# Where the first MLP's activation lives and which engine makes its low half, in tiles 3 to 5

## The chip, the cores and the metric

One core of a Trainium2 chip. The metric is the device time of one execution in microseconds (us), the median of several runs.

## What is computed

An attention layer (4 batches, 8 heads, 576 positions, head size 64, causal, with a bias from a running sum) gives 2304 rows of 512 numbers. Two MLPs follow. What matters here is the first:

```python
h = x @ w_in                                          # 512 -> 2048
g = np.maximum(h, 0.0) + np.log1p(np.exp(-np.abs(h)))
return (g @ w_out).astype(np.float32)                 # 2048 -> 512
```

The second MLP has the same shape, with a rational function of h in place of g.

## The kernel before

Every product is made to fp32 accuracy from three matmuls of rounded operands. An operand is split into a high half (a rounded copy) and a low half (the rest), and the products high-high, high-low and low-high are summed. So each activation needs both halves before the second product of the MLP can start.

The 2304 rows of the first MLP are cut into six tiles (`T1`, line 17): T = 0 and 1 have 256 rows, T = 2 to 5 have 448. The hidden dimension has 16 blocks `ff` of 128. A unit is one block of one tile. For the first MLP (`ph == 0`) a unit passes through these steps:

- `stage_a_` (L650 to L665): 12 matmuls (L662, L663, L664) write h, 128 x 448, into one bank of PSUM. `hsel` (L669) names the ring the bank comes from. There are eight banks: four `acc`, two `h`, two `at` (L92).
- `stage1_` (L743 on): ScalarE takes |h|, its exponential and its logarithm into the SBUF tile `e` (L749 to L751, two buffers). VectorE adds max(h, 0) and writes the sum over `e` (L752). With this instruction the bank of h is free.
- `stage3_` (L783): ScalarE rounds `e` into `gh` (L788), and GpSimd subtracts: `gl` = `e` - `gh` (L789). Both have three buffers.
- `stage_b` (L684): three units later, 12 matmuls (L698, L699, L700) multiply `gh` and `gl` with the second weight and add into the four `acc` banks. In the tile T = 5 two of the four are taken from `at` (`open_acc`, L675).

Beside this run two other streams. Attention is one list of steps (`s1`, `s2`, `t1`, `t2`, `pv`), of which `gap` (L900) emits a share with each unit; the last of it belongs to the units of T = 3. It takes its banks from `at`. In a step VectorE reduces the scores and adds the mask (L300, L306, L309), ScalarE exponentiates (L313), VectorE makes the reciprocal of the sum (L314, L315), GpSimd multiplies with it (L316, tiles `PA` and `P`), TensorE transposes (L377, L388, L393), and ScalarE and VectorE split the result into halves (L363, L364). L283 and L284 make low halves of q and k; in the last segment of attention L284 is put on GpSimd. In T = 4 and 5 the weights of the second MLP are converted (`conv2_a`, `conv2_b`), one per unit in T = 4: a DMA brings 64-bit numbers (`raw`), GpSimd scales them (L532), VectorE puts the bits together in `tc` (L533, L534, L535), ScalarE rounds them (L539), GpSimd subtracts (L540). `raw` and `tc` have two buffers each. `split_x_` (L632) makes the halves of a tile's input, `xs`.

Each engine works through its own instructions in a fixed order. That order comes from a list scheduler, which goes by program order and by the priorities set with `ahead` and `early` (`PRIO`, `P_ST1`, `P_ST3` and others, L45 to L52). The units of the first MLP that the change touches are these:

```python
units += [(ph, T, ff) for ph in range(2) for T in range(2 - 2 * ph, 6) for ff in range(NF)]
```

Of the kernel before, what the change touches and what calls it, by code (L numbers as in the profile page):

```python
# [12 lines left out]
ALU = mybir.AluOpType  # L13
# [16 lines left out]
H_ONLY = 5  # L30
# [25 lines left out]
def moe_chain_kernel(ctx, tc, qk0, qk, vv, s0, s, w1, w2, ab, out):  # L56
    nc = tc.nc
# [31 lines left out]
    def tmp_tile(tag, bufs, shape=(128, TMAX), dt=F32):  # L89
        return sb.tile(list(shape), dt, tag=tag, bufs=bufs, name=tag)  # L90
# [10 lines left out]
    def early(by_region):  # L101
        return ahead(by_region[region[0]])

    def f(ap):
        return ap.bitcast(F32)
# [544 lines left out]
    def stage_a_(u):  # L650
        ph, T, ff = u
        bk = bank(hsel(ph, T, ff))
        n = TILES[ph][T][1]
        h = bk[:, 0:n]
        if ph == 0:
            wh, wl = w1_t[ff][:, 0:512], li_t.pop((T, ff, 0))
        else:
            wh, wl = w2_t[ff, 0]
        for k in range(KD):
            xh, xl = xs_t[ph, T, k]  # L660
            cs = slice(k * 128, (k + 1) * 128)
            nc.tensor.matmul(h, wh[:, cs], xh, start=(k == 0), stop=False)  # L662
            nc.tensor.matmul(h, wh[:, cs], xl, start=False, stop=False)  # L663
            nc.tensor.matmul(h, wl[:, cs], xh, start=False, stop=(k == KD - 1))  # L664
        h_t[u] = h  # L665
# [1 line left out]
    hcnt = [0]  # L667

    def hsel(ph, T, ff):  # L669
        if ph == 0 or (T == 0 and ff < H_ONLY):  # L670
            return "h"
        hcnt[0] += 1
        return ("h", "at")[hcnt[0] % 2]
# [62 lines left out]

    e_t = {}

    def stage1(u):
        with early(P_ST1):  # L740
            stage1_(u)

    def stage1_(u):  # L743
        ph, T, ff = u
        h = h_t[u]
        n = TILES[ph][T][1]
        if ph == 0:
            e = tmp_tile("e", 2)[:, 0:n]
            nc.scalar.activation(e, h, AF.Abs)  # L749
            nc.scalar.activation(e, e, AF.Exp, scale=-1.0)  # L750
            nc.scalar.activation(e, e, AF.Ln, bias=1.0)  # L751
            nc.vector.scalar_tensor_tensor(e, h, 0.0, e, op0=ALU.max, op1=ALU.add)  # L752
            e_t[u] = e
        else:
            a = tmp_tile("e", 2)[:, 0:n]
            t = tmp_tile("PA", 3, (128, n))
            w = tmp_tile(*(("P4", 1), ("tc", 2), ("tmp", 1), ("tc", 2))[(T * NF + ff) % 4], (128, n))
            nc.scalar.activation(a, h, AF.Abs)
            nc.scalar.activation(w, a, AF.Identity, scale=babs[:, 1:2], bias=babs[:, 0:1])  # L759
            nc.scalar.activation(t, h, AF.Identity, scale=nega[:, 3:4], bias=nega[:, 2:3])  # L760
            nc.gpsimd.tensor_tensor(w, w, a, op=ALU.mult)  # L761
            nc.vector.tensor_tensor(t, t, h, op=ALU.mult)
            nc.vector.scalar_tensor_tensor(t, t, nega[:, 1:2], h, op0=ALU.add, op1=ALU.mult)
            e_t[u] = (a, t, w)
# [14 lines left out]
    def stage3(u):  # L779
        with early(P_ST3):  # L780
            stage3_(u)

    def stage3_(u):  # L783
        g = e_t.pop(u)
        n = TILES[u[0]][u[1]][1]
        gh = tmp_tile("gh", 3, dt=F32R)[:, 0:n]
        gl = tmp_tile("gl", 3, dt=F32R)[:, 0:n]
        nc.scalar.activation(gh, g, AF.Copy)  # L788
        nc.gpsimd.tensor_tensor(gl, g, f(gh), op=ALU.subtract)  # L789
        g_t[u] = (gh, gl)  # L790


    if True:
# [129 lines left out]
        for i in range(NU + LAGS[1]):  # L923
            at_bank[0] = second_bank if i < 8 + LAGS[0] else at_only
            u = units[i] if i < NU else None
            region[0] = 0 if i < 32 else 1 if i < 96 else 2
            if u is not None:
                ph, T, ff = u
                if ph == 0 and T == 0:
                    conv1_to(c1_pos[ff, 0] + 1)  # L930
                stage_a(u)
                gap(i, 0)
                stage1(u)
                with ahead(C2_OFF):
                    while c2_open:
                        conv2_b()
                if ph == 0 and T == 0:
                    e = HF - 1 if ff < HF else NF - 1
                    conv1_to(c1_pos[min(ff + 2, e), 0] + 1)
                    if ff >= e + 1 - HF:  # L940
                        conv1_to(c1_pos[ff, 1] + 1)
                    if ff == e:
                        conv1_to(c1_pos[e, 1] + 1)
                if ph == 0 and T == 1 and ff < HF:
                    conv1_to(NF + int((ff + 1) * C1_RATE), False)
                for k in splits.get(i, ()):
                    split_x(*k)
# [91 lines left out]
```

## Time and profile before

| what | value |
|---|---|
| time, median of 3 runs | 1121.24 us (1118.62 to 1124.24) |
| the profiled execution's own time | 1123.89 us |
| its span, first to last instruction | 1122.1 us |
| TensorE busy (matmul) | 1040.2 us, 93% |
| VectorE busy | 834.8 us, 74% |
| ScalarE busy | 823.4 us, 73% |
| GpSimd busy | 574.9 us, 51% |
| mean granted TensorE clock | 0.969 |

In the rows, PE is TensorE's matmuls, PEld its weight loads, DVE is VectorE, ACT is ScalarE, POOL is GpSimd, and L752 is line 752 of the kernel before. By the first h matmul of each tile, T = 2 runs from about 253.4 to 378.0 us of the span, T = 3 to 541.5, T = 4 to 619.1, T = 5 to 703.4, and the second MLP fills the rest. A matmul's busy time contains the overlap with its neighbours, so a busy TensorE is not one at its peak; what counts are the stretches in which it stood idle, and what ended them.

### The profile page before, as it was taken

The page shows a single profiled execution, that of the slowest core. Times are in us where ns is not written, and L with a number is a line of the kernel's source. Part 1 is how long each engine was busy: PE and PEld are TensorE (multiplying, and loading weights), DVE is VectorE, ACT ScalarE, POOL GpSimd, SP SyncE. Part 2 cuts the span into 40 slices and gives each one's busy share as a digit, 9 for nine tenths or more (in the row PEclk, how much of TensorE's full clock was granted, in tenths as well). Part 3 has the DMA queues.
Part 4 walks back from the last instruction along what each step waited for, and adds up shares of the span by engine and source line. Part 5 has one row for each costly group of instructions (what it writes and reads, how often), then busy time and mean ns, then how long its engine had stood idle before and what let it go on. Part 6 is the DMA issues. An engine that isn't in the chain of part 4 may idle for free.

```text
span 1122.1 us, 17899 instructions
## 1 busy us (share of the span) xinstructions
PE 1040.2 (93%) x5732; PEld 934.1 (83%) x5732; DVE 834.8 (74%) x1874; ACT 823.4 (73%) x1735; POOL 574.9 (51%) x605
## 2 busy tenths in 40 slices
PE   3678898889999999999999999899999999999998
PEld 2477688889888888777999888799999999999997
DVE  6899898787777678787377667877667676776765
ACT  6677768777788687776646545678878887887885
POOL 3656466573334454543267566644554455454443
PEclk8589899999999999999999999999999999999999
DMA  6554556456555464431566886600001010000000
GB/s 221 169 173 168 171 201 221 152 192 193 161 160 165 129 184 161 134 99 52 161 220 227 292 268 231 205 7 29 29 15 43 1 47 11 29 29 1 30 1 28
DMA packets 70494, 140.54 MB, mean 125 GB/s; under 512 B 8384, under 2 KB 23904, under 8 KB 70400
## 3 DMA queue, kind: packets, MB, share of 16 engines
q1 hardware_dynamic: 68000, 135.37, 36.7%
q10 hardware_dynamic: 2400, 4.03, 1.5%
q8 instruction: 45, 0.74, 0.3%
q14 instruction: 49, 0.40, 0.1%
HBM read 112.66 MB, written 22.61 MB: 121 GB/s over the span
## 4 chain that ended last, share of the span: by engine, by line
PE 43%; DVE 7%; DMA 4%; POOL 3%; issue 2%; ACT 2%; SPq 0%; POOLq 0%; DVEq 0%; ACTq 0%
PE acc L707 6%; PE acc L706 6%; PE acc L705 6%; DMA raw<-in_w_dram 4%; PE h L662 4%; PE h L664 4%; PE h L663 4%; PE at L662 3%; PE at L664 3%; PE at L663 3%; DVE tc L534 1%; DVE tc L535 1%; DVE tc L533 1%; POOL w2l L540 1%; PE at L419 1%
## 5 line engine op out<-in xcount | busy, mean ns | idle before, releaser
L789 POOL TENSOR_TENSOR gl<-e,gh 128x448 fp32r<-128x448 f32 (+1 forms) x96 | 105.7, 1102 | 79.5 <-ACT gh L788 76.6
L662 PE MATMUL h<-xs,w1h 128*128 128x448 f32 (+1 forms) x384 | 134.1, 349 | 8.0 <-DVE e L752 5.6
L663 PE MATMUL h<-xs,w1h 128*128 128x448 f32 (+1 forms) x384 | 133.3, 347 | 2.2 <-DVE xs L632 2.2
L664 PE MATMUL h<-xs,w1l 128*128 128x448 f32 (+1 forms) x384 | 131.4, 342 | 0.4 <-DMA w1l<-l_d 0.4
L699 PE MATMUL acc<-gl,w1h 128*128 128x448 f32 (+1 forms) x352 | 120.3, 342 | 1.7 <-POOL gl L789 1.7
L698 PE MATMUL acc<-gh,w1h 128*128 128x448 f32 (+1 forms) x352 | 120.6, 343 | 0.0
L700 PE MATMUL acc<-gh,w1l 128*128 128x448 f32 (+1 forms) x352 | 120.1, 342 | 0.0
L316 POOL TENSOR_SCALAR PA<-PA,stat 128x384 f32<-128x384 f32 (+3 forms) x112 | 73.7, 662 | 83.8 <-DVE stat L315 35.1
L707 PE MATMUL acc<-w2h,gl 128*128 128x512 f32 x288 | 113.3, 394 | 0.4 <-POOL gl L789 0.4
L705 PE MATMUL acc<-w2h,gh 128*128 128x512 f32 x288 | 113.2, 393 | 0.4 <-ACT gh L788 0.4
L706 PE MATMUL acc<-w2l,gh 128*128 128x512 f32 x288 | 113.1, 393 | 0.0
L789 POOL TENSOR_TENSOR gl<-PA,gh 128x384 fp32r<-128x384 f32 x96 | 99.4, 1035 | 5.1 <-issue 2.9
L761 POOL TENSOR_TENSOR tc<-tc,e 128x384 f32<-128x384 f32 x48 | 51.3, 1068 | 99.0 <-ACT tc L759 99.0
L788 ACT ACTIVATE gh<-e 128x448 fp32r<-128x448 f32 (+1 forms) x96 | 50.0, 521 | 66.3 <-DVE e L752 61.2
L662 PEld LDWEIGHTS h<-xs,w1h 128*128 128x128 f32 x384 | 74.4, 194 | 14.7 <-DVE e L752 7.9
L663 PEld LDWEIGHTS h<-xs,w1h 128*128 128x128 f32 x384 | 74.3, 194 | 7.1 <-DVE xs L632 3.9
L364 DVE TENSOR_TENSOR ptl<-at,pth 128x384 fp32r<-128x384 f32 (+2 forms) x108 | 60.8, 568 | 25.9 <-ACT pth L363 24.2
L533 DVE TENSOR_SCALAR tc<-raw 128x512 int32<-128x512 int32 x64 | 44.4, 698 | 47.0 <-POOL raw L532 22.8
L664 PEld LDWEIGHTS h<-xs,w1l 128*128 128x128 f32 x384 | 73.9, 192 | 3.8 <-DMA w1l<-l_d 0.6
L363 ACT ACTIVATE pth<-at 128x384 fp32r<-128x384 f32 (+2 forms) x108 | 53.4, 499 | 29.8 <-PE at L393 18.2
L313 ACT ACTIVATE PA<-PA,stat 128x384 f32<-128x384 f32 (+3 forms) x112 | 63.8, 570 | 15.3 <-DVE stat L300 11.7
L532 POOL TENSOR_SCALAR raw<-raw 128x512 f32<-128x512 f32 x64 | 51.1, 800 | 42.9 <-DMA raw<-in_w_dram 41.4
(206 smaller groups left out, 3316.6 us busy)
## 6 DMA issues: line engine op xcount, KB each, us to landing
w1l<-l_d SPq DMA_DIRECT2D x148, 256.0 KB
raw<-in_w_dram SPq DMA_DIRECT2D x64, 512.0 KB
raw<-in_qk_dram SPq DMA_DIRECT2D x32, 384.0 KB
l_d<-w1l SPq DMA_DIRECT2D x32, 256.0 KB
R<-in_vv_dram SPq DMA_DIRECT2D x16, 320.0 KB
raw<-in_qk_dram SPq DMA_DIRECT2D x8, 576.0 KB
out_dram<-yb SPq DMA_DIRECT2D x18, 256.0 KB
w_d<-PA SPq DMA_DIRECT2D x16, 256.0 KB
```

The source lines that it names most:

```text
L313: nc.scalar.activation(pt[:, 0:n], pt[:, 0:n], AF.Exp, bias=mn, scale=-1.0, accum_out=stat[:, i, 1:2])
L316: nc.gpsimd.tensor_scalar(pt[:, 0:n], pt[:, 0:n], stat[:, i, 2:3], 1.0, op0=ALU.mult, op1=ALU.mult)
L662: nc.tensor.matmul(h, wh[:, cs], xh, start=(k == 0), stop=False)
L663: nc.tensor.matmul(h, wh[:, cs], xl, start=False, stop=False)
L664: nc.tensor.matmul(h, wl[:, cs], xh, start=False, stop=(k == KD - 1))
L698: nc.tensor.matmul(o, wh[:, cs], gh, start=first and not both, stop=False)
L699: nc.tensor.matmul(o, wh[:, cs], gl, start=False, stop=False)
L700: nc.tensor.matmul(o, wl[:, cs], gh, start=False, stop=last and (not both or m % 2 == 1))
L705: nc.tensor.matmul(acc[m], gh[:, cs], wh, start=first, stop=False)
L706: nc.tensor.matmul(acc[m], gh[:, cs], wl, start=False, stop=False)
L707: nc.tensor.matmul(acc[m], gl[:, cs], wh, start=False, stop=last)
L789: nc.gpsimd.tensor_tensor(gl, g, f(gh), op=ALU.subtract)
```

## The change

For T = 2, 3 and 4 of the first MLP, VectorE writes the activation over h in its PSUM bank, ScalarE rounds it from there into `gh`, and VectorE subtracts `gh` from it to make `gl`. GpSimd has no part in these 48 units any more. In T = 4 the banks of h come in turn from `at` and `h`; in T = 2, 3 and 5 from `h` alone, as before.

```diff
     def hsel(ph, T, ff):
-        if ph == 0 or (T == 0 and ff < H_ONLY):
+        if (ph == 0 and T != 4) or (ph == 1 and T == 0 and ff < H_ONLY):
             return "h"
         hcnt[0] += 1
         return ("h", "at")[hcnt[0] % 2]
...
+    def in_bank(u):
+        return u[0] == 0 and 2 <= u[1] <= 4
...
-            nc.vector.scalar_tensor_tensor(e, h, 0.0, e, op0=ALU.max, op1=ALU.add)
-            e_t[u] = e
+            g = h if in_bank(u) else e
+            nc.vector.scalar_tensor_tensor(g, h, 0.0, e, op0=ALU.max, op1=ALU.add)
+            e_t[u] = g
...
         nc.scalar.activation(gh, g, AF.Copy)
-        nc.gpsimd.tensor_tensor(gl, g, f(gh), op=ALU.subtract)
+        eng = nc.vector if in_bank(u) else nc.gpsimd
+        eng.tensor_tensor(gl, g, f(gh), op=ALU.subtract)
```

## Rows read from the trace of the kernel before

**Rows 1.** T = 2 to 5: length, busy PE, PEld, DVE, ACT, POOL, PE clock, DMA.

```profile
253.40:378.00 124.60, 123.88 (x731) 110.56 (x731) 94.36 (x291) 100.09 (x229) 47.42 (x57) 1.00 0.56 170
378.00:541.50 163.50, 155.13 (x922) 133.93 (x921) 122.59 (x366) 121.23 (x272) 74.85 (x84) 1.00 0.39 122
541.50:619.10 77.60, 77.60 (x385) 71.95 (x384) 46.04 (x57) 43.92 (x83) 47.20 (x42) 1.00 0.65 216
619.10:703.40 84.30, 78.57 (x378) 69.60 (x377) 58.17 (x71) 43.46 (x82) 52.20 (x47) 1.00 0.79 263
```

**Rows 2.** TensorE's largest wait in T = 3: us in total, times, longest.

```profile
PE at L393 <- POOL P L316: 5.5, 7, 1.8
```

**Rows 3.** TensorE's waits in T = 5: us in total, times, longest.

```profile
PE h L662 <- DVE e L752: 2.9, 3, 1.9
PE h L663 <- DVE xs L632: 2.0, 4, 0.7
```

**Rows 4.** Instruction groups over the whole span: busy us, mean ns, idle before.

```profile
L789 POOL TENSOR_TENSOR gl<-e,gh 128x448 fp32r<-128x448 f32 x64 | 78.1, 1221 | 66.0 <-ACT gh L788 64.7
...
L752 DVE SCALAR_TENSOR_TENSOR e<-h,e 128x448 f32<-128x448 f32 x64 | 39.5, 618 | 16.0 <-ACT e L751 15.6
...
L788 ACT ACTIVATE gh<-e 128x448 fp32r<-128x448 f32 x64 | 36.9, 576 | 59.5 <-DVE e L752 54.4 <-PE acc L700 3.1 <-PE h L664 1.1
L749 ACT ACTIVATE e<-h 128x448 f32<-128x448 f32 x64 | 34.4, 537 | 19.9 <-PE h L664 17.1 <-POOL gl L789 1.7 <-POOL PA L316 0.9
```

**Rows 5.** VectorE's longest wait in T = 2 and 3: us, times, longest.

```profile
DVE ptl L364 <- ACT pth L363: 22.3, 30, 3.4
```

**Rows 6.** Timeline near the end of T = 2: one gl, and the bank's next matmul.

```profile
370.68 1.62 POOL L789 TENSOR_TENSOR gl<-e,gh 128x448 fp32r<-128x448 f32 x1
...
373.11 0.37 PE L662 MATMUL h<-xs,w1h 128*128 128x448 f32 x1
```

**Rows 7.** Timeline in T = 3: GpSimd's queue ahead of one wait of TensorE.

```profile
415.69 1.16 POOL L789 TENSOR_TENSOR gl<-e,gh 128x448 fp32r<-128x448 f32 x1
416.83 0.74 POOL L316 TENSOR_SCALAR P<-P,stat 128x576 f32<-128x576 f32 x1
...
417.62 0.55 PE L393 MATMUL at<-ident,P 128*128 128x128 f32 x3 [0.75 <-POOL P L316]
```

**Rows 8.** Timeline in T = 3: GpSimd's gl beside VectorE, and TensorE's longest wait.

```profile
482.23 1.55 POOL L789 TENSOR_TENSOR gl<-e,gh 128x448 fp32r<-128x448 f32 x1
...
482.76 1.57 DVE L534 SCALAR_TENSOR_TENSOR tc<-raw,tc 128x512 int32<-128x512 int32 x1
484.25 0.15 DVE L315 RECIPROCAL stat<-stat 128x1 f32<-128x1 f32 x1
...
485.37 0.33 PE L393 MATMUL at<-ident,P 128*128 128x128 f32 x1 [1.82 <-POOL P L316]
```

**Rows 9.** Timeline in T = 4: the conversion on VectorE, with and without gl beside it.

```profile
590.27 1.36 DVE L533 TENSOR_SCALAR tc<-raw 128x512 int32<-128x512 int32 x1 [1.37 <-POOL w2l L540]
591.67 0.69 DVE L534 SCALAR_TENSOR_TENSOR tc<-raw,tc 128x512 int32<-128x512 int32 x1
...
594.60 0.43 DVE L533 TENSOR_SCALAR tc<-raw 128x512 int32<-128x512 int32 x1 [0.66 <-POOL w2l L540]
...
590.19 1.16 POOL L789 TENSOR_TENSOR gl<-e,gh 128x448 fp32r<-128x448 f32 x1
```

**Rows 10.** Timeline where T = 5 begins: VectorE, GpSimd, and TensorE's first matmuls.

```profile
617.79 1.37 DVE L533 TENSOR_SCALAR tc<-raw 128x512 int32<-128x512 int32 x1 [1.65 <-POOL PA L540]
619.08 0.61 DVE L632 TENSOR_TENSOR xs<-x,xs 128x448 fp32r<-128x448 f32 x1
...
617.71 1.17 POOL L789 TENSOR_TENSOR gl<-e,gh 128x448 fp32r<-128x448 f32 x1
...
619.13 0.36 PE L662 MATMUL h<-xs,w1h 128*128 128x448 f32 x1
...
624.60 0.36 PE L698 MATMUL acc<-gh,w1h 128*128 128x448 f32 x1
```

## The prediction

> **What bounds the kernel now.** The page says that TensorE is busy 93% of the span and no other engine over 74%. That is a mean over stages, so I first read the busy times stage by stage, for the four tiles T = 2 to 5 that the change touches or borders on [rows 1]. The reader should subtract TensorE's busy time from the length of each stretch. T = 2 leaves 0.72 us idle of 124.60, T = 4 leaves nothing of 77.60, T = 3 leaves 8.37 of 163.50 and T = 5 leaves 5.73 of 84.30. The clock stood at 1.00 of its full 2.4 GHz in all four. So a faster or slower VectorE or GpSimd changes T = 2 and T = 4 only if it makes TensorE wait where it now doesn't, and all that can be won in these tiles is 8.37 + 5.73 = 14.1 us.
>
> Next I read what ended the idle time. In T = 3 it is mostly GpSimd's scaling of the softmax rows, `P` at L316: 5.5 us in 7 waits [rows 2]. In T = 5 it is VectorE: 2.9 us until the activation freed a bank of h, and 2.0 us until it had made the low half of the tile's input [rows 3]. Neither is directly the instruction that the change moves. The move matters through the queues: GpSimd's `gl` may stand in front of `P`, or slow VectorE beside it, and VectorE's new `gl` may stand in front of what makes `P` ready.
>
> **What goes from GpSimd.** 48 subtractions of 128 x 448 (three tiles of 16 units) at 1.221 us [rows 4], 58.6 us of GpSimd. GpSimd is busy at most 61% in any of these stretches (47.20 of 77.60) [rows 1], so this is worth only what stood behind it. Two places can be priced.
>
> In T = 3 at 415.69 us `gl` took 1.16 us, `P` started when it was over, and TensorE then waited 0.75 us for `P` [rows 7]. Without `gl` that wait can go: at most -0.75.
>
> At 482.23 us `gl` ran beside VectorE's L534, which took 1.57 us; the reciprocal L315 came behind it, `P` behind that, and TensorE waited 1.82 us, its longest wait for `P` [rows 2, 8]. The same L534 with no `gl` beside it took 0.69 [rows 9]. So VectorE reads two SBUF operands slower while GpSimd subtracts: 1.57 - 0.69 = 0.88 us less there.
>
> In T = 4 the same happens in every unit to the conversion: L533 took 1.36 us beside `gl` and 0.43 without it [rows 9]. That shortens the conversion loop by up to 0.93 us per unit, but TensorE never waits in T = 4 [rows 1], so it is worth nothing there. It shows where T = 5 begins. There L533 took 1.37 us beside a `gl`, and the low halves of the next tile's input (L632) queue behind it on VectorE [rows 10]. TensorE needed from 619.13 to 624.60 us, 5.47 us, for 12 matmuls that take 2.43 at the pace of T = 4 (77.60 us for 384, 0.202 each) [rows 1, 10]. The stall is 3.0 us. Of this 1.37 - 0.43 = 0.94 goes for certain if L533 starts where it does now, and all 3.0 if the conversion loop has come earlier by that much during T = 4. I take 2, in the middle of these ends: the loop has 16 units in which to gain, but can't overtake the activations that it shares VectorE with. For the 2.9 us that T = 5 waits for the activation [rows 3], behind the same loop, I take 1 of 2.9, as its DMAs are issued somewhat earlier; T = 5 itself keeps its GpSimd `gl`.
>
> **What VectorE takes on.** 48 subtractions that read h from PSUM and `gh` from SBUF. The nearest row is L752, which reads the same two places at the same size: 0.618 us [rows 4]; 48 x 0.618 = 29.7 us, some 9.9 in each tile. VectorE's busy time goes from 94.36 to at most 104.3 of 124.60 in T = 2, from 122.59 to 132.5 of 163.50 in T = 3, from 46.04 to 56 of 77.60 in T = 4 [rows 1]; it stays below TensorE in each.
>
> It also takes on a wait: `gl` needs ScalarE's `gh`, and VectorE runs in order, so the next reductions, reciprocals and halves of attention stand behind it. The row for such a wait is L364, the same kind of subtraction behind the same kind of ScalarE copy: 30 waits of 22.3 / 30 = 0.74 us in T = 2 and 3 [rows 5]. So each `gl` costs VectorE 0.62 us at the least and 1.36 at the most. In T = 4 the wait falls into time that VectorE now spends waiting for GpSimd (1.37 us in the row) [rows 9], so it costs nothing; without that cover it would be 16 x 0.74 = 11.8 us of an engine that still has 20 to spare. In T = 2 TensorE has 0.72 us of idle time in 124.60, so the chains through VectorE reach it in time nearly always; I take 0. In T = 3 they are often late. The last segment of attention has 16 parts that make a `P` (8 of kind H, 8 of LH, L450), one per unit or so, and 7 times TensorE waited for one [rows 2]. A `gl` falls between scores and `P` in perhaps a third of the units, 5 of 16, and half of these have no slack: 2.5 x 0.62 = 1.5 us. The ends are 0 and 16 x 1.36 = 21.8.
>
> **The bank.** It is held until `gl` is done, not until L752 is. With two banks the next use is two units later. The tightest place I found is at the end of T = 2: a `gl` ended on GpSimd at 372.30 us and the bank's next matmul started at 373.11, 0.81 us later [rows 6]. VectorE's `gl` is half as long, so as a rule it ends no later than GpSimd's. I take 0. In T = 4, where units follow each other at TensorE's full pace, the four banks give the turn twice the time.
>
> **Other edits.** VectorE writing over h in PSUM isn't in this trace. Reading shows what the place costs: 0.618 us with h from PSUM against 0.61 for L632 with SBUF alone [rows 4, 10]; ScalarE reads 448 columns in 0.537 from PSUM and 0.576 from SBUF [rows 4], so `gh` gains 48 x 0.04 = 1.9 us of ScalarE. I take nothing for the write, with -0.04 to +0.04 as its ends, 2 us of VectorE in all either way, off the path. The Trainium skill (Perfetto Trace Analysis, Optimizing Scalar/DVE Operations) speaks against this: it gives VectorE an overhead of about 125 ns on PSUM against 60 on SBUF. By that the 48 writes would cost 48 x 65 ns = 3.1 us of VectorE more, an estimate, a third of it in T = 3; no row here shows such a difference on reads. `e` comes free earlier, at L752; the waits for it are small (1.7 us for 64 units) [rows 4]. The second MLP's turn of banks is not moved, since T = 4 takes 16 steps of a turn of two. No DMA is moved.
>
> **The sum.** T = 2: 0. T = 3: -0.75 - 0.88 + 1.5 = -0.1. T = 4: 0. T = 5: -2 - 1 = -3. In all -3.1 us. The profiled execution took 1123.89 us (span 1122.1 and 1.8 around it), 2.65 above the median of 1121.24; from the median, 1118. A measurement of this kernel can tell about 0.5%, 5.6 us, from no change.
>
> **The rivals.**
>
> *Faster: GpSimd's queue was what made T = 3 late.* With GpSimd free `P` follows its reciprocal at once, and VectorE's attention work no longer slows beside `gl`. Then the 5.5 us of waits for `P` [rows 2] and 4.5 of the 5.73 idle in T = 5 [rows 1] go: -10, 1111. For it: rows 7 and 8 show both effects. Against it: GpSimd has 54% idle time in T = 3, and only one of the 7 waits has `gl` directly ahead of `P` in the stretches that I read.
>
> *Slower: VectorE's new `gl` stands in front of the reciprocals in T = 3.* Each `P` waits for L315 on VectorE, and `gl` with its wait for ScalarE is put ahead of it. It decides from the point at which nearly all 16 `gl` of the tile are on that path: 12 x (0.62 + 0.37, half the wait) = 11.9 us, less the 1.6 and 3.0 won elsewhere: +7, 1128. For it: VectorE is at 75% in T = 3 and most of TensorE's waits there go back to it or to GpSimd behind it. Against it: the same tile has 41 us in which VectorE is idle, into which 16 short instructions fit.
>
> *The bank comes back late.* In T = 2 and 3 there are still two banks of h. If `gl` on VectorE ends over 0.81 us later than it did on GpSimd wherever the units run close together, as in the last four of each tile, TensorE waits some 0.5 us in each of these 8: +4, so +1 in all, 1122. Against it: elsewhere attention lies between two units. The edit could also do nothing at all, if every `gl` falls into idle time of either engine; then it is 1121, near my own forecast.
>
> **How the numbers follow.** My forecast 0.45, most of it within 0.5% (0.41) and some faster (0.04). Faster 0.28. Slower 0.20. The late bank 0.07, 0.06 of it within 0.5% and 0.01 slower. That makes faster 0.32, same 0.47, slower 0.21. The range runs from 1109, just beyond the faster rival, to 1129, just beyond the slower one; what it leaves out is T = 3 losing all 21.8 us, or both tiles losing all their 14.1 us of idle time.
>
> **What would show it.** Right: the groups show `gl` on VectorE near 0.62 us, 48 times; T = 4 again 77.6 us long; T = 3 within 3 us of 163.5; the first 12 matmuls of T = 5 in about 3.5 us, and L533 near 0.43 in T = 4. Wrong: T = 3 shorter by 5 or longer by 5, with waits for `P` gone or grown; waits of h's first matmul for L789's successor on VectorE in T = 2 or 3; or a T = 4 in which TensorE stands idle.

## The result, and the profile after

The median fell from 1121.24 us (1118.62 to 1125.07, 5 runs) to 1109.4 us (1108.49 to 1113.32, 5 runs): a ratio of 0.9902, with a 95% interval of 0.9883 to 0.9922. Run again in the study below, the same kernel came to 0.9942 (0.9922 to 0.9963). The two intervals just touch, at 0.992, so the change gives some 0.6% to 1.0%. The sign that I forecast is right and the size is not: 1118.0 stood for a gain of 3.1 us, and 6 to 12 were measured. No change within 0.5%, which I held the likeliest, is not what the first measurement shows, and the repeat's interval only reaches into it. The first time lies in the stated range by 0.4 us, at the end that the faster rival set and not my own sum. Rare executions take far longer (1677 us of the kernel before, 2130 and 2206 in the profiled ones of e1 and e8): they are in no ratio or median here, and e1 and e8 have no stage lengths.

The profiled execution took 1113.32 us, of which 1111.5 is its span, 10.6 less than the span of before. These are the busy times stage by stage of the kernel after, in the columns of [rows 1]: T = 2 to 5, each from its first h matmul to that of the next.

```profile
250.63:373.25 122.62, 122.58 (x731) 110.57 (x729) 98.63 (x306) 100.02 (x230) 29.54 (x43) 1.00 0.57 173
373.25:532.83 159.58, 154.22 (x922) 133.53 (x920) 127.50 (x382) 121.26 (x272) 56.56 (x68) 1.00 0.41 125
532.83:610.48 77.65, 77.65 (x385) 72.09 (x384) 46.09 (x76) 44.67 (x84) 26.70 (x27) 1.00 0.69 228
610.48:692.79 82.31, 78.70 (x377) 71.51 (x376) 54.71 (x68) 43.45 (x81) 49.46 (x45) 0.98 0.76 258
```

Beside [rows 1], T = 2 is 1.98 us shorter, T = 3 3.92, T = 4 the same, T = 5 1.99. That makes 7.8 of the 10.6. The other 2.8 lie ahead of T = 2 (250.63 us for 253.40), where TensorE's order of instructions is the same in both kernels. There the length goes with the granted clock of TensorE: 0.865 of its full 2.4 GHz on the mean before, 0.877 after, and 0.979 in experiment e4 below, which reached T = 2 some 6 us earlier. So I compare the sums of T = 2 to 5 and leave the part ahead of them out. The second MLP took 418.7 us in both.

GpSimd lost 17.9, 18.3 and 20.5 us of busy time in T = 2, 3 and 4. VectorE gained 4 to 5 us in T = 2 and 3, and nothing in T = 4 (46.09 for 46.04), though it took on some 10 us in each. The groups of VectorE's instructions over the whole span, after (busy us, mean ns, idle before), tell what each cost.

```profile
L756 DVE SCALAR_TENSOR_TENSOR h<-h,e 128x448 f32<-128x448 f32 x40 | 25.1, 628 | 8.6 <-ACT e L754 8.3
...
L794 DVE TENSOR_TENSOR gl<-h,gh 128x448 fp32r<-128x448 f32 x40 | 24.7, 618 | 5.5 <-ACT gh L792 5.2
...
L756 DVE SCALAR_TENSOR_TENSOR e<-h,e 128x448 f32<-128x448 f32 x16 | 9.8, 616 | 1.2 <-ACT e L754 1.2
```

The new subtraction takes 618 ns, as the row it was priced by [rows 4]; the other 8, in the banks of `at`, take 619. Writing over h in PSUM takes 628 ns where the 16 units of T = 5 still write to SBUF in 616. The groups of ScalarE show `gh` at 540 ns from PSUM and 580 from SBUF:

```profile
L792 ACT ACTIVATE gh<-h 128x448 fp32r<-128x448 f32 x40 | 21.6, 540 | 23.7 <-DVE h L756 13.5 <-PE acc L700 7.5 <-PE at L664 1.8
...
L792 ACT ACTIVATE gh<-e 128x448 fp32r<-128x448 f32 x16 | 9.3, 580 | 24.7 <-DVE e L756 24.7
```

What pays for VectorE's subtractions in T = 4 is the conversion beside them. The mean of L533 there fell from 860 to 508 ns and that of L534 from 1144 to 757, since GpSimd no longer makes `gl` while they run, as [rows 9] had it for single ones. In e9 below, with such a subtraction back on GpSimd, they are 810 and 1022.

TensorE's waits in T = 3, after (us in total, times, longest), answer to [rows 2]:

```profile
PE at L393 <- POOL P L316: 4.2, 6, 1.0
PE at L393 <- DVE x L431: 0.9, 1, 0.9
PE at L393 <- DVE ptl L364: 0.2, 1, 0.2
```

The waits for `P` fell by 1.3 us only, 4.2 for 5.5. The one that I took 0.75 us from [rows 7] is still there. This is the timeline of the kernel after, at the same place in the order:

```profile
410.11 0.61 DVE L794 TENSOR_TENSOR gl<-h,gh 128x448 fp32r<-128x448 f32 x1
...
410.64 0.13 DVE L314 TENSOR_SCALAR stat<-stat 128x1 f32<-128x1 f32 x1
...
410.81 0.16 DVE L315 RECIPROCAL stat<-stat 128x1 f32<-128x1 f32 x1
...
411.17 0.74 POOL L316 TENSOR_SCALAR P<-P,stat 128x576 f32<-128x576 f32 x1 [1.20 <-DVE stat L314]
...
411.97 0.66 PE L393 MATMUL at<-ident,P 128*128 128x128 f32 x4 [0.72 <-POOL P L316]
```

GpSimd stood idle for 1.20 us ahead of `P`, so it wasn't late. The reciprocal was: it now stands behind VectorE's own `gl`. The longest wait of before [rows 8] did go, but in another way than I had it. Timeline of the kernel after, at that place:

```profile
474.39 0.15 DVE L315 RECIPROCAL stat<-stat 128x1 f32<-128x1 f32 x1
...
474.47 0.96 DVE L533 TENSOR_SCALAR tc<-raw 128x512 int32<-128x512 int32 x1
...
475.24 0.80 POOL L316 TENSOR_SCALAR P<-P,stat 128x576 f32<-128x576 f32 x1
...
475.46 1.12 DVE L534 SCALAR_TENSOR_TENSOR tc<-raw,tc 128x512 int32<-128x512 int32 x1
```

In [rows 8] the reciprocal came after L534. Now it comes ahead of L533 and L534: the order on VectorE has changed. The list scheduler laid out the rest of the work anew once 48 instructions had changed engines. L534 itself still takes 1.12 us here, not the 0.69 that I counted on.

Three stretches of T = 3 show what the new order does to TensorE: from the first transpose (L393) of the `P` before this one to the first of its own, from there to the first of the next, and from the first of the tile's last `P` to the tile's end. They are given in the columns of [rows 1], for the kernel before and then for the kernel after.

```profile
470.30:485.37 15.07, 12.73 (x73) 10.56 (x73) 13.36 (x38) 9.34 (x23) 8.00 (x9) 1.00 0.43 141
485.37:497.80 12.43, 11.95 (x72) 10.23 (x72) 11.00 (x34) 10.49 (x24) 6.08 (x8) 1.00 0.33 103
530.99:541.50 10.51, 10.51 (x58) 9.64 (x59) 5.47 (x13) 6.91 (x16) 1.17 (x1) 1.00 0.22 76
```

```profile
464.66:477.38 12.72, 11.82 (x71) 9.99 (x72) 10.82 (x33) 9.25 (x21) 6.25 (x7) 1.00 0.51 163
477.38:490.73 13.35, 13.35 (x78) 11.51 (x79) 11.67 (x38) 10.35 (x24) 5.94 (x8) 1.00 0.33 102
523.97:532.83 8.86, 8.86 (x50) 8.10 (x50) 5.11 (x14) 6.36 (x16) 0.00 (x0) 1.00 0.32 90
```

The first shrank by 2.35 us. The second grew by 0.92, with 78 matmuls in it for 72, and the third shrank by 1.65, with 50 for 58: the new order has matmuls beside attention that used to stand behind it. That is 3.1 of the 3.92 us.

Last, the begin of T = 5 in the kernel after, where [rows 10] stood:

```profile
607.21 0.43 DVE L533 TENSOR_SCALAR tc<-raw 128x512 int32<-128x512 int32 x1 [1.36 <-POOL PA L540]
...
607.55 0.62 DVE L632 TENSOR_TENSOR xs<-x,xs 128x448 fp32r<-128x448 f32 x1
...
610.48 0.37 PE L662 MATMUL h<-xs,w1h 128*128 128x448 f32 x1
```

The first L632 now comes 2.9 us ahead of TensorE's first matmul, where it was level with it, and the 12 matmuls of the first unit took 3.15 us instead of 5.47 [rows 10]. TensorE's waits in T = 5, after (us in total, times, longest), answer to [rows 3]; what became of the long one is told in the last section.

```profile
PE h L662 <- DVE e L756: 2.5, 1, 2.5
PE at L700 <- DMA w1l<-l_d: 0.6, 1, 0.6
PE h L663 <- DVE xs L632: 0.4, 1, 0.4
```

### The profile page after: what moved, and what is told of

Its sections match the earlier page's. It is cut to its first block, busy times and chain, and to the rows that moved or that the text cites. A ratio compares the mean times of both kernels' runs of the same rounds, so it can differ in the third digit from the quotient of the medians.

```text
span 1111.5 us, 17851 instructions
## 1 busy us (share of the span) xinstructions
PE 1035.3 (93%) x5732; PEld 932.7 (84%) x5732; DVE 841.3 (76%) x1922; ACT 823.2 (74%) x1735; POOL 514.8 (46%) x557
## 4 chain that ended last, share of the span: by engine, by line
PE 68%; DVE 15%; DMA 5%; POOL 5%; ACT 4%; issue 3%; SPq 0%; POOLq 0%; DVEq 0%; ACTq 0%
PE h L662 6%; PE h L663 6%; PE h L664 6%; PE acc L707 6%; PE acc L706 6%; PE acc L705 6%; PE at L419 4%; PE acc L699 3%; PE acc L698 3%; PE acc L700 3%; PE at L662 3%; PE at L664 3%; PE at L663 3%; DMA raw<-in_w_dram 3%; PE at L319 2%
## 5 line engine op out<-in xcount | busy, mean ns | idle before, releaser
L662 PE MATMUL h<-xs,w1h 128*128 128x448 f32 (+1 forms) x352 | 122.4, 348 | 7.7 <-DVE e L756 5.5
L663 PE MATMUL h<-xs,w1h 128*128 128x448 f32 (+1 forms) x352 | 121.7, 346 | 0.6 <-DVE xs L632 0.6
L664 PE MATMUL h<-xs,w1l 128*128 128x448 f32 (+1 forms) x352 | 120.3, 342 | 0.0
L662 PEld LDWEIGHTS h<-xs,w1h 128*128 128x128 f32 x352 | 68.1, 193 | 13.2 <-DVE e L756 7.0
L533 DVE TENSOR_SCALAR tc<-raw 128x512 int32<-128x512 int32 x64 | 41.8, 659 | 46.6 <-POOL raw L532 20.9
L364 DVE TENSOR_TENSOR ptl<-at,pth 128x384 fp32r<-128x384 f32 (+2 forms) x108 | 60.6, 568 | 17.9 <-ACT pth L363 16.2
L699 PEld LDWEIGHTS acc<-gl,w1h 128*128 128x128 f32 x352 | 67.6, 192 | 5.7 <-POOL gl L794 2.6
L663 PEld LDWEIGHTS h<-xs,w1h 128*128 128x128 f32 x352 | 68.4, 194 | 4.2 <-DVE xs L632 1.2
L664 PEld LDWEIGHTS h<-xs,w1l 128*128 128x128 f32 x352 | 68.1, 193 | 2.9
L698 PEld LDWEIGHTS acc<-gh,w1h 128*128 128x128 f32 x352 | 67.6, 192 | 3.0
```

The source lines that it names most:

```text
L698: nc.tensor.matmul(o, wh[:, cs], gh, start=first and not both, stop=False)
L699: nc.tensor.matmul(o, wh[:, cs], gl, start=False, stop=False)
```

## The experiments

Three readings were open. The gain could come from GpSimd's time (it is free, and VectorE runs faster beside it), from the new order that the scheduler makes, or from the place of the activation in PSUM. Ratios are to the kernel before, run beside each batch on the same chip. There were four batches on four chips (e1 to e4; r_after, e6, e9 and e10; e7, e8 and e11; e12), and the medians of before were 1118.3 to 1119.2. Stage lengths are those of one profiled execution each. Diffs are against the changed kernel, and `...` in them stands for lines left out: e1, e2, e4, e10, e11 and e12 also take two banks in T = 4, by the edit that is shown under e6. The names e1 to e3 count tiles from one, so that e1_tile3 is T = 2.

**The changed kernel again (r_after)**, with no edit.

> The changed kernel again, beside the others on one chip. The three tiles alone gave 0.12, 0.30 and 0.12%, 0.54% together (6 us); the whole change gave 0.98%. If the tiles add up: 0.993 to 0.995 of before. If the tiles help each other: 0.990 again.

Measured: 0.9942 (0.9922 to 0.9963), median 1112.79. T = 2 to 5 took 123.1, 160.4, 77.7 and 79.1 us, 440.3 in all, against 450.0 before [rows 1] and 442.2 in the first profile.

**GpSimd kept as busy as before (e9_pool_still).** GpSimd subtracts as well, on the SBUF tile that nobody reads any more.

```diff
+    e_x = {}
...
+            e_x[u] = e
...
+        if in_bank(u):
+            e = e_x.pop(u)
+            nc.gpsimd.tensor_tensor(e, e, f(gh), op=ALU.subtract)
```

> The changed kernel with GpSimd kept as busy as before: it also subtracts the rounded half from the logarithm that is left in the SBUF tile, which nobody reads, and holds that tile as long as before. The order of the other four engines is that of the changed kernel. If GpSimd's relief (its queue, and VectorE's slower reads beside it) is the gain: the time of before, 0.998 to 1.002, with T = 3 near 163 us and 12 matmuls in 5.5 us where T = 5 begins. If it is the new order and the earlier low half: the changed kernel's time, T = 3 near 159.6.

Measured: 1.0016 (1.0003 to 1.003), median 1120.48. The whole gain is gone. On TensorE, VectorE, ScalarE and SyncE the order of instructions is that of the changed kernel, and so is GpSimd's but for the 48 that were added, so order and load come apart here. VectorE's 48 subtractions stay as well, so this is more load than the kernel before had. The added group on GpSimd, and then the busy times stage by stage in T = 2 to 5, of e9:

```profile
L799 POOL TENSOR_TENSOR e<-e,gh 128x448 f32<-128x448 f32 x48 | 56.9, 1186 | 62.4 <-ACT gh L794 60.3 <-PE acc L699 1.8
```

```profile
248.87:373.50 124.63, 123.44 (x730) 110.34 (x729) 102.59 (x307) 101.43 (x234) 48.96 (x59) 1.00 0.56 171
373.50:533.56 160.06, 154.68 (x921) 133.57 (x920) 129.00 (x381) 121.22 (x272) 74.94 (x84) 1.00 0.41 124
533.56:611.21 77.65, 77.65 (x385) 72.19 (x384) 51.67 (x70) 40.97 (x77) 44.15 (x41) 1.00 0.66 212
611.21:697.92 86.71, 80.31 (x377) 71.68 (x375) 59.08 (x73) 46.43 (x87) 51.88 (x49) 0.96 0.79 259
```

T = 3 keeps its gain (160.06 us for 163.50) with GpSimd at 74.94 us of work, where it had 74.85 before: the new order alone is enough there. T = 2 is back where it was (124.63 for 124.60), and the same instructions of VectorE took 102.59 us in it, for 98.63 in the kernel after. T = 5 is longer than before (86.71 for 84.30). Against the repeat of the changed kernel T = 5 lost 7.6 us, T = 2 1.5, and T = 3 won 0.3: 8.8 us, near the 8.3 that the two ratios differ by (0.0074 of 1118.5). Against the first profile of the changed kernel, whose T = 5 was longer, the sum is 6.9. Where T = 5 begins, the timeline of e9 shows how:

```profile
612.25 1.13 POOL L799 TENSOR_TENSOR e<-e,gh 128x448 f32<-128x448 f32 x1
...
612.32 1.34 DVE L533 TENSOR_SCALAR tc<-raw 128x512 int32<-128x512 int32 x1 [1.60 <-POOL PA L540]
...
613.58 0.61 DVE L632 TENSOR_TENSOR xs<-x,xs 128x448 fp32r<-128x448 f32 x1
...
614.24 0.74 PE L663 MATMUL h<-xs,w1h 128*128 128x448 f32 x1 [2.66 <-DVE xs L632]
```

L533 again takes 1.34 us beside a subtraction on GpSimd, the half of the input comes late, TensorE waits 2.66 us and then runs at a lower clock (the last section). The first 12 matmuls took 8.7 us.

**No low half in T = 2 to 4 (e10_no_gl).** No engine subtracts; the second product takes `gh` in place of `gl`. The activation is in SBUF and the banks are as before.

```diff
...
-            g = h if in_bank(u) else e
+            g = e
...
+        if in_bank(u):
+            gl = gh
...
```

> No low half in T = 2 to 4: the second matmul reads the high half again (this part of the computation is left out), banks as before. GpSimd is relieved and VectorE takes on nothing, so this is the most that the move can give. If VectorE's 29.7 us cost something on the path: faster than the changed kernel by 1.5 to 5 us. If they cost nothing: within 1 us of it.

Measured: 0.9933 (0.9908 to 0.9957), median 1111.89, no different from the changed kernel's 0.9942. So VectorE's 29.7 us of new work cost nothing that can be measured; the two intervals leave room for some 3 us. T = 3 took 160.36 us without it and 159.58 and 160.4 with it. At the place of the 0.72 us wait shown above, TensorE waited 0.18 here. So the `gl` ahead of the reciprocal may well cost 0.54 there, though e10 has another order too; in the sum it doesn't show.

**The engine without the place (e4_engine).** The activation stays in SBUF, VectorE subtracts, two banks.

```diff
...
-            g = h if in_bank(u) else e
+            g = e
```

> The engine alone: VectorE makes the low half in T = 2 to 4, but from the SBUF tile, with h's bank freed as before and two banks in T = 4. If GpSimd's relief is all that counts: 1109 to 1111, as the changed kernel. If it matters that the subtraction reads PSUM: it slows beside GpSimd now, 1.3 to 1.5 us in place of 0.62 where they overlap, and slows GpSimd's P; half of the gain, 1114 to 1117.

Measured: 0.9946 (0.9923 to 0.9969), median 1113.09; T = 2 to 5 took 440.9 us. That is the changed kernel's gain without the activation in PSUM. The group of the subtraction in e4:

```profile
L794 DVE TENSOR_TENSOR gl<-e,gh 128x448 fp32r<-128x448 f32 x48 | 31.6, 659 | 6.5 <-ACT gh L792 6.3
```

Its mean is 41 ns above that in the bank. Five of the 48 make the whole difference: they took 739 to 1355 ns, each beside a GpSimd instruction, and the others 604 to 627, among them eight beside GpSimd's scaling of the softmax rows. In the bank none went over 625, neither in the kernel after nor in e9, where 43 of the 48 ran beside a GpSimd instruction. These are the subtractions of e4, and then those of e9 in the banks of `h` (ns: least, median, most).

```profile
L794 DVE TENSOR_TENSOR gl<-e,gh x48: 604/618/1355, 255.6 to 612.8; 128x448 fp32r<-128x448 f32 x48
```

```profile
L796 DVE TENSOR_TENSOR gl<-h,gh x40: 605/618/625, 258.5 to 620.2; 128x448 fp32r<-128x448 f32 x40
```

This agrees with the Trainium skill (SBUF — State Buffer, Who interferes with whom): a VectorE instruction with two inputs from SBUF contends with a GpSimd instruction that reads SBUF, and one with at most one SBUF input, outside the modes in which VectorE uses two ports, doesn't. L533 has one input from SBUF and was slowed all the same, 1.36 us for 0.43 [rows 9]; no run here shows in which mode it ran.

**Two banks in T = 4 (e6_two_banks).**

```diff
-        if (ph == 0 and T != 4) or (ph == 1 and T == 0 and ff < H_ONLY):
+        if ph == 0 or (T == 0 and ff < H_ONLY):
```

> The change with two banks in T = 4 as before. The place in PSUM holds a bank until the low half is done, 1.5 to 4 us longer than before, and in T = 4 of before the bank came free 1 to 3 us ahead of its next use. If the four banks matter: TensorE waits in T = 4, which becomes 80 to 90 us long in place of 77.7. If not: 77.7 and the changed kernel's time.

Measured: 0.9966 (0.9946 to 0.9985), median 1115.7. T = 4 became 79.23 us long. TensorE's only wait in T = 4 of e6:

```profile
PE h L662 <- DVE gl L794: 1.3, 1, 1.3
```

The bank came back late once, by 1.3 us. So the four banks are worth some 1.6 us to T = 4 once the activation holds its bank until `gl` is done. T = 5 took 84.60, with 6.0 us of waiting for the activation, though its code and TensorE's order in it are those of the changed kernel; why is open. The two ratios' intervals overlap, so the whole time barely shows e6 apart from the changed kernel.

**One tile further in the bank (e7_tile6).**

```diff
-        return u[0] == 0 and 2 <= u[1] <= 4
+        return u[0] == 0 and 2 <= u[1] <= 5
```

> The change carried on into T = 5, in the bank, where only two banks of h are left. GpSimd's subtraction is the only thing beside the conversion loop that it does in T = 5. If its relief counts there as it did at the begin of T = 5: T = 5 at 76 to 79 us in place of 79 to 82, 0.988 to 0.992 of before. If the two banks, held longer, decide: TensorE waits for h as in the two-bank run (79.2 us for T = 4), T = 5 at 82 to 86, 0.993 to 0.998.

Measured: 0.9943 (0.9924 to 0.9963), median 1112.3: the same as the changed kernel. T = 5 took 83.4 us; TensorE's waits in it, of e7, are mostly for the bank:

```profile
PE h L662 <- DVE gl L794: 3.7, 3, 2.5
PE h L663 <- DVE xs L632: 0.9, 1, 0.9
```

**T = 2 to 5 on VectorE, from SBUF (e11_sbuf_to_tile6)**, with two banks.

```diff
...
-        return u[0] == 0 and 2 <= u[1] <= 4
+        return u[0] == 0 and 2 <= u[1] <= 5
...
-            g = h if in_bank(u) else e
+            g = e
```

> VectorE makes the low half in T = 2 to 5, from the SBUF tile, banks as before. Relief in T = 5 without a bank held longer: T = 5 at 76 to 79 us, T = 2 and 3 as in the run of the engine alone (123.6 and 160.5), 0.988 to 0.992. If VectorE, which has the conversion loop and slower reads beside GpSimd, is what T = 5 waits for: 0.994 to 0.997.

Measured: 0.9909 (0.9888 to 0.9929), median 1108.02; T = 5 took 78.65 us. On the same chip e7, with T = 5 in the bank and 83.4 us long, had a median 4.3 us higher. But e4, where GpSimd still makes `gl` in T = 5, took 79.06 there: what T = 5 itself gains in e11 is not shown.

**T = 2 and 3 in the bank, T = 4 and 5 from SBUF (e12_mixed)**, all on VectorE, two banks:

```diff
...
-        return u[0] == 0 and 2 <= u[1] <= 4
+        return u[0] == 0 and 2 <= u[1] <= 5
...
-            g = h if in_bank(u) else e
+            g = h if u[0] == 0 and u[1] in (2, 3) else e
```

> VectorE makes the low half in T = 2 to 5: in T = 2 and 3 in the bank, as the change has it, in T = 4 and 5 from the SBUF tile, with two banks as before. If the stages add up as the profiles have them (T = 2 at 122.6 to 123.1, T = 3 at 159.6 to 160.4, T = 4 at 77.7, T = 5 at 78.6): 0.989 to 0.992 of before, no worse than the run from SBUF to T = 5 (0.9909) and perhaps 1 us better. If the order that the scheduler finds counts for more than the stages' parts: anything from 0.989 to 0.996.

Measured: 0.9911 (0.9891 to 0.9931), median 1108.62; T = 5 took 80.2 us. e11 and e12 beat the kernel before by 0.9%. They lie 0.3% under the 0.9942 of the changed kernel's repeat, but the intervals overlap, and its first 0.9902 is as low as theirs: that they beat the changed kernel is not shown. Both do without the four banks, with T = 4 at 77.6 and 77.7 us.

**One tile alone (e1_tile3, e2_tile4, e3_tile5)**: the change for T = 2 and for T = 3, each with two banks throughout, and for T = 4 with its four.

```diff
...
-        return u[0] == 0 and 2 <= u[1] <= 4
+        return u[0] == 0 and u[1] == 2
```

> The change in T = 2 alone. My own account (TensorE has 0.7 us of idle time in T = 2, so nothing can be won there): 1121, T = 2 at 124.6 us. The rival 'GpSimd freed' has no wait for P of any size there either: 1120 to 1121. If the 2.0 us by which T = 2 is shorter in the changed kernel (122.6 for 124.6) belong to its own units: 1119, and T = 2 at 122.6.

> The change in T = 3 alone. My own account (what GpSimd gives, VectorE takes): T = 3 within 1 us of 163.5, 1121. The rival 'GpSimd freed': the 3.9 us by which T = 3 is shorter in the changed kernel (159.6 for 163.5) come again, 1117, with fewer waits for P.

> The change in T = 4 alone, with its four banks. My own account: T = 4 stays at 77.6 us, T = 5 begins with 12 matmuls in 3.3 to 3.5 us in place of 5.5: 1118 to 1119. The rival 'GpSimd freed': the same place and also the later waits of T = 5, -4.5: 1116.5. T = 2 and 3 have the order of the kernel before here, so their lengths are a second reading of before: 124.6 and 163.5 if those were typical.

Measured: 0.9988 (0.9969 to 1.0006), 0.997 (0.9953 to 0.9987) and 0.9988 (0.997 to 1.0005). Together they make 0.54%, about the 0.58% of the whole change's repeat, with intervals too wide to say more; only that of T = 3 leaves out no change. With T = 3 alone changed, T = 3 took 159.4 us and T = 2, 4 and 5 were 124.9, 77.7 and 84.4, as before. With T = 4 alone changed, its length stayed at 77.7 and T = 5 fell to 81.7; T = 2 and 3, where TensorE has the order of before, took 124.9 and 162.7. So T = 3's gain is its own and T = 4's is the next tile's; for T = 2 alone there is no stage length.

**All tiles, the small ones too (e8_all).**

```diff
-        return u[0] == 0 and 2 <= u[1] <= 4
+        return u[0] == 0
```

> The change in all six tiles, four banks in T = 4 alone. In T = 0 and 1 VectorE is the busiest engine (217 us of the first 253), so the low half costs there what it takes: 32 x 0.41 = 13 us on VectorE, slower than before by 3 to 10 us in these tiles if VectorE bounds them; faster by 1 to 3 if GpSimd's queue does.

Measured: 0.9937 (0.9915 to 0.996), median 1112.54: nothing more from T = 0, 1 and 5. Of the 3 to 10 us of loss or the 1 to 3 of gain that I expected in T = 0 and 1, the whole time shows neither.

## Why the prediction was right or wrong

**T = 2: forecast 0, measured -1.5 to -2.0 us.** The failed step is that only the 0.72 us in which TensorE is shown idle could be won. The same 731 matmuls were busy for 123.88 us before and 122.58 after [rows 1], so their busy time held pauses that no view shows as idle. In e9, with GpSimd's load put back under the same order, T = 2 is 124.63 again, and its matmuls were busy for 123.44 us: that load made the pauses. VectorE's instructions took 2.8 to 4.0 us more in sum beside it than in the two profiles of the changed kernel; that the pauses come from these I argue and haven't shown. Load may not be all of it: over the profiles T = 2 takes 122.6 to 123.1 us in the five with the activation in the bank (the changed kernel twice, e6, e7, e12), 123.6 to 124.0 in the three that have it in SBUF (e4, e10, e11), and 124.6 to 124.9 in before, e2, e3 and e9. e4 and e6 differ there by the place alone, and so do e11 and e12, 0.65 and 0.81 us in single profiles; but VectorE's order changed with the place, so that these two aren't told apart.

**T = 3: forecast -0.1, measured -3.1 to -3.9.** All three terms were wrong. The -0.75 for the wait at [rows 7] is 0: the wait stayed, now behind VectorE's `gl`. The +1.5 for `gl` ahead of the reciprocals is 0 in the sum, by e10, though perhaps 0.54 at that one place. For the -0.88 at [rows 8] the wait did end, through the reciprocal's new place, not through a faster L534. Between that transpose and the one ahead of it the time fell from 15.1 us to 12.7, in the changed kernel and in e9 alike; 0.9 went again in the next step, and 1.6 more came at the tile's end, again in both. The failed step lies under all three terms: I moved instructions within an order that I held fixed. e9 shows that the order, with GpSimd as loaded as before, gives 2.6 to 3.4 us, against the 162.7 of e3 and the 163.50 of before. An earlier low half is not the reason, since in T = 3 of before none of TensorE's waits was for `gl`. What relief alone would give in the old order was not tried.

**T = 4: forecast 0, measured 0.** TensorE has no idle time there in either kernel, and VectorE's wait and subtraction fall into time that the conversion gave up.

**T = 5: forecast -3, measured -2.0 and -5.2.** The begin was right. 2 us were forecast of a 3.0 us stall, and 2.3 were won (3.15 us for the first 12 matmuls, 5.47 before; 3.97 in e3). L533 ran in 0.43 us as the row said, and e9, which puts GpSimd's load back, takes 8.7 us there: it is GpSimd's subtraction that made VectorE late. The later part is the term that was mis-sized: -1 for an earlier activation is too small when TensorE's clock holds and too large when it doesn't: 79.10 us in the repeat, 82.31 in the first profile, of one and the same kernel.

**The bank: forecast 0, right for T = 2 and 3**, where no wait for `gl` is among TensorE's waits, and right in that T = 4 needed the other banks: with two it waits 1.3 us (e6), and T = 5 in the bank waits 3.7 (e7).

**The prices: right.** 618 ns for the subtraction; the write over h 12 ns more, within the 40 that I gave as ends. By the figures that the prediction took from the Trainium skill (Perfetto Trace Analysis, Optimizing Scalar/DVE Operations) it would have been 65 ns more: the runs don't bear this out for VectorE. For ScalarE the same section has an access on PSUM 42 ns cheaper than on SBUF, and that agrees with the 40 measured (540 and 580).

**The rivals.** The slower one's mechanism exists, at one place and for at most the 0.72 us waited there. The faster one, GpSimd's queue, gave 1111, nearest to the median of 1109.4, and its cause is half right: GpSimd's load is what e9 takes the whole gain back with. But it names the wrong place. The waits for `P` that it wanted gone are 4.2 us in the changed kernel, in e9 and in e10; the load counts in T = 2 and at T = 5. One reading was off, with nothing resting on it: GpSimd's highest share is that of T = 5, 62% (52.20 of 84.30) [rows 1], not 61%.

## What to carry to other kernels

In a kernel whose order a list scheduler makes, moving work to another engine is two changes: a new load and a new order. They are told apart by leaving the new order and putting the old load back as work that nobody reads. Where TensorE's busy share is near 100%, its busy time is still no floor: 731 matmuls lost 1.3 us of it. An instruction on VectorE that takes all its inputs from SBUF is worth pricing by what GpSimd does beside it: L533, with one such input, took 0.43 us or 1.36, and L534, with two, 0.69 or 1.57 [rows 8, 9].

## What the runs showed of the hardware that I had not expected

A wait of a few microseconds can cost twice, though it doesn't always. In T = 5 of the first profile of the changed kernel TensorE waited 2.52 us for a bank of h. Its matmuls then ran slower for some time. Here are TensorE's timeline there, and the window around it in the columns of [rows 1], with a mean granted clock of 0.72:

```profile
663.61 0.47 PE L662 MATMUL h<-xs,w1h 128*128 128x448 f32 x1 [2.52 <-DVE e L756]
...
664.33 0.56 PE L662 MATMUL h<-xs,w1h 128*128 128x448 f32 x1
...
667.29 0.57 PE L664 MATMUL h<-xs,w1l 128*128 128x448 f32 x1
```

```profile
662.00:668.00 6.00, 4.39 (x14) 3.95 (x15) 3.95 (x7) 2.69 (x5) 2.27 (x3) 0.72 0.85 291
```

From 664.33 to 667.29 us the 9 matmuls start 0.37 us apart, not 0.20: some 1.5 us lost behind a wait of 2.52. In the repeat the same wait was 1.00 us and the clock stayed at 1.00; 1.5 us less of waiting and 1.5 of clock are 3.0 of the 3.2 us between the two lengths of T = 5. The repeat's T = 5 in the columns of [rows 1], and its waits for the activation there (us in total, times, longest):

```profile
610.20:689.30 79.10, 77.26 (x377) 70.15 (x376) 54.16 (x68) 43.16 (x80) 48.87 (x45) 1.00 0.82 267
```

```profile
PE h L662 <- DVE e L756: 1.3, 2, 1.0
```

In e9 the wait of 2.66 us was followed by a stretch at 0.50, the lower of the two levels, 1.2 GHz (the window of e9, same columns):

```profile
614.20:620.40 6.20, 5.43 (x13) 3.78 (x14) 5.86 (x9) 1.73 (x5) 2.44 (x3) 0.50 0.51 168
```

So the begin of T = 5 in e9 took 8.7 us where before, with a stall in smaller pieces [rows 3, 10] and the clock at 1.00, it took 5.47. The length of one wait doesn't decide it in these runs. In e10 a wait of 1.99 us was followed by a stretch at 0.50, while in T = 5 of e6 a wait of 2.86 us left the clock at 1.00. This is TensorE's timeline of e6 there, and the window from it on:

```profile
678.03 0.47 PE L662 MATMUL h<-xs,w1h 128*128 128x448 f32 x1 [2.86 <-DVE e L756]
```

```profile
678.00:684.00 6.00, 5.97 (x29) 5.56 (x30) 3.52 (x5) 5.38 (x10) 3.72 (x4) 1.00 0.79 249
```

The T = 5 of one kernel differed by 3.2 us between two profiles, and with it how much of the change one run shows.
